# Channel attention with a squared-ReLU network behind it: a third buffer for rectified pairs and for split scores, nine for tokens, fewer for weights; all plain stores on SP's queue; a scheduler that assumes longer transfers

## The chip, the cores and the metric

One core of a Trainium2 chip runs the whole program. The metric is the device time of one execution in microseconds (us). PE is TensorE with its matmuls, PEld its weight loads, DVE is VectorE, ACT is ScalarE, POOL is GpSimd and SP is SyncE, which computes nothing here and issues transfers. All five work through their own instructions strictly in order, so an instruction that waits for a semaphore holds everything behind it on its engine.

## The reference

```
B, N, C = 4, 6080, 256
qn = q / (norm(q, axis=1) + 1e-06);  kn = k / (norm(k, axis=1) + 1e-06)
s = kn.transpose(0, 2, 1) @ qn / tau              # per batch 256 x 256
a = softmax(s, axis=-1)
x = (v @ a).reshape(24320, 256)
h = x @ w_in                                      # 256 -> 2048
g = maximum(h, 0) ** 2
out = g @ w_out                                   # 2048 -> 256
```

## The kernel before

**The work.** Attention is folded into the first weight: for each of the four batches `fold` multiplies the batch's 256 x 256 attention matrix by `w_in`, so the tokens `v` go straight into the network. Numbers are split into a high and a low part (`split`: a cast, then a subtraction on DVE), and each product is three matmuls, in the trace 128 x 128 weights by 512 or 480 columns. The tokens of a batch are cut into six chunks (five of 2 x 512 tokens, one of 2 x 480), 24 in all; the hidden layer is cut into eight blocks `j`. A chunk and a block make a "quad" (`quads`, 192 of them), and a quad's first layer is done with seven products instead of eight (`m1` to `m7`, weights `wt`, tokens `vt`).

**One quad.** The order of products on PE is m1, m7, some second-layer products, m6, m2, more of the second layer, m5, m4, more, m3 (`steps_of`). m1 goes into a PSUM bank of ring `h`, and ACT copies it to a bank `x` (`COPY x<-h`) before m6 may add to the first bank; m6's copy goes to `z`; m7 takes the second `h` bank and ACT copies it to SBUF (`m7`, shown as `m`). ACT rectifies m2 and m3 into a pair (ring `s`), DVE's line 704 adds `m7` to m4 and m5 and rectifies them (ring `s`, or `D` in the blocks that spare a product in the second layer too). A pair is squared on ACT, then split into high and low (ring `g2`), which the second layer reads one or two quads later with weights `wo`. The blocks in `GROUPS` also form sums of weights and of pairs (`load_later`, `split_later`, `run_later`: tiles `wo<-wod_M...`, `hl`, `kq`, results `uM...`), and the results leave through `outT<-uM` stores on SP's queue.

**Weights by way of DRAM.** A batch's folded weights are combined and split on ACT and DVE into a tile of ring `wt` (`combine`), stored to DRAM (`wsc`), and loaded again into the same ring of three buffers for each chunk (`load_wt`). Second-layer weights and the sums of them are prepared once (`wop`, `wos`, `wod`) and loaded for each quad into ring `wo`. While a batch's chunks run, the next batch's scores are computed: `kq` tiles are loaded, squared on ACT, added to `acc` by a DMA that accumulates (POOL's queue), split into ring `hl`, and multiplied.

**The order.** Nothing is ordered by hand. `Plan.order` simulates five engines (SP and POOL as "S" and "G", which only issue) and takes at each step the operation that is ready: for PE, SP and POOL the one with the smallest key, for ACT and DVE the one with the earliest due time. An operation starts only if its tiles' rings have a free buffer. Two estimates of a transfer go in: `delay` (from which due times are worked out backward) and, in the forward pass, `link` and `done`, the time at which readers may start. Operations that ACT or DVE can do (casts) go to whichever takes them first. So numbers in `RINGS` and in the estimates move instructions on all engines.

```
                    if e in "SG":
                        link = max(link, now + 0.8) + op.size / 330.0
                        done = link + 1.4
...
    RINGS = {"kq": 4, "g2": 3, "D": 3, "hl": 2, "t4": 1, "s": 2, "sq": 2, "wo": 6, "wt": 3, "vt": 8, "v": 1, "tt": 1,
```

Of the kernel before, what the change touches and what calls it, by code (L numbers as in the profile page):

```python
# [24 lines left out]
class Plan:  # L25
# [19 lines left out]
    def add(self, key, engines, fn, r=(), w=(), size=0):  # L45
        op = Op()
        op.engines, op.fn, op.key, op.size, op.n = engines, fn, key, size, len(self.ops)
        op.deps, op.users, op.tiles = set(), set(), set()
        for t in r:
            if t in self.writer:  # L50
                op.deps.add(self.writer[t])
            self.readers.setdefault(t, []).append(op)
        for t in w:
            op.deps.update(self.readers.pop(t, ()))
            if t in self.writer:
                op.deps.add(self.writer[t])
            self.writer[t] = op
        op.deps.discard(op)
        for t in (*r, *w):
            if t[0] in self.ring_of and t[0] not in op.tiles:  # L60
                op.tiles.add(t[0])
                self.users[t[0]].append(op)
        self.ops.append(op)
        return op
# [2 lines left out]
        return min(op.engines.values())  # L67

    def delay(self, op, e):
        return 2.2 + op.size / 330.0 if e in "SG" else self.LAT[e]  # L70

    def order(self):

# [21 lines left out]
        for op in reversed(ops):  # L95
            due = op.due if "P" in op.engines else end
            e = next(iter(op.engines))
# [22 lines left out]
        link = 0.0  # L120
        now = 0.0
        out = []
        seq = 0
        while events:
            now = heapq.heappop(events)
            while events and events[0] <= now + 1e-9:
                heapq.heappop(events)
            while ends and ends[0][0] <= now + 1e-9:
                op = heapq.heappop(ends)[2]
                for name in op.tiles:  # L130
                    open_[name] -= 1
                    if not open_[name] and name in live:
                        free[live.pop(name)] += 1
            progress = True
            while progress:
                progress = False
                for e in engines:
                    if at[e] > now + 1e-9:
                        continue
                    while head < len(pe) and pe[head] in begun:  # L140
                        head += 1
                    place = pe[head].key if head < len(pe) else 1e9
                    best = None
                    for op in waiting[e]:
                        if op.ready > now + 1e-9 or op.key > place + self.ahead[e]:
                            continue
                        rank = (op.key, op.n) if e in "PSG" else (
                            op.due + self.shy.get(e, 0.0) * (len(op.engines) > 1), op.n)
                        if best is not None and rank >= best[0]:
                            continue  # L150
                        need = {}
                        for name in op.tiles:
                            if name not in live:
                                need.setdefault(self.ring_of[name], []).append(turn[name])
                        if any(free[ring] < len(n) or ring not in self.loose and max(n) >= served[ring] + len(n)
                               for ring, n in need.items()):
                            continue
                        best = rank, op
                    if best is None:
                        continue  # L160
                    op = best[1]
                    for x in op.engines:
                        waiting[x].remove(op)
                    begun.add(op)
                    for name in op.tiles:
                        if name not in live:
                            live[name] = self.ring_of[name]
                            free[live[name]] -= 1
                            served[live[name]] += 1
                    op.begun = now  # L170
                    out.append((op, e))
                    at[e] = now + op.engines[e]
                    done = at[e] + self.LAT.get(e, 0.0)
                    if e in "SG":
                        link = max(link, now + 0.8) + op.size / 330.0
                        done = link + 1.4
                    seq += 1
                    heapq.heappush(events, at[e])
                    heapq.heappush(events, done)
                    heapq.heappush(ends, (done, seq, op))  # L180
                    for u in op.users:
                        u.left -= 1
                        u.ready = max(u.ready, done)
                        if not u.left:
                            for x in u.engines:
                                waiting[x].append(u)
                            heapq.heappush(events, u.ready)
                    progress = True
# [23 lines left out]
def tile_channel_attention_relu2_ffn(ctx, tc, kq, vT, tau, w_in, w_out, outT):  # L212
# [12 lines left out]
    G = 2  # L225
# [3 lines left out]
    GROUPS = ((0, 1, 2), (4, 5))  # L229
    SJ = sum(GROUPS, ())  # L230
    BIG = 3.4028234663852886e38
    RINGS = {"kq": 4, "g2": 3, "D": 3, "hl": 2, "t4": 1, "s": 2, "sq": 2, "wo": 6, "wt": 3, "vt": 8, "v": 1, "tt": 1,
             "m7": 2, "uM1": 1, "uM5": 1, "uM6": 1, "uM7": 1, "acc": 1, "s_acc": 1, "zq": 1, "e": 2, "den": 2,
             "aT": 1, "y": 3, "nm": 2,
             "h": 2, "x": 1, "z": 1, "o00": 1, "o01": 1, "o10": 1, "o11": 1}
    plan = Plan(RINGS, {"P": 0.7, "A": 1.2, "V": 1.2, "S": 2.0, "G": 2.0}, ("h",))
    add = plan.add
# [18 lines left out]
    def get(name, shape=None, dtype=F32):  # L256
        if name not in made:
# [5 lines left out]
            else:  # L263
                pool = small if ring in ("acc", "s_acc", "zq", "e", "den", "aT", "y", "nm") else work
                made[name] = pool.tile(shape, dtype, name=ring, tag=name[-1] if ring in ("aT", "y") else ring,
                                       bufs=1 if ring == "y" else RINGS[ring])
        return made[name]
# [29 lines left out]
    def load(key, out, in_, r, w, size):  # L297
        add(key, {"S": 0.45}, lambda e: nc.sync.dma_start(out=out(), in_=in_()), r, w, size)

    def store(key, out, in_, r, w, size, e="G"):  # L300
        add(key, {e: 0.45 if e == "S" else 1.0},
            lambda e: (nc.sync if e == "S" else nc.gpsimd).dma_start(out=out(), in_=in_()), r, w, size)

# [55 lines left out]
    def decode_w_in(key, g, lead=0.9):  # L359
        Wn = decode(key, "in", g, "sq" if g else "t4", lead)  # L360
        win[0, g] = Wn
        store(key, lambda: dtile(("wins", g), [P, 4, GW]), lambda: made[Wn], [(Wn, 0)], [(("wins", g), 0)], 512)
# [723 lines left out]
```

## Time and profile before

| | |
|---|---|
| time, median of 3 runs | 2133.39 us (2130.94 to 2135.16) |
| the profiled execution's own time | 2129.49 us |
| its span on the core | 2127.6 us |
| PE busy | 2097.1 us, 99% of the span |
| DVE, ACT, POOL busy | 1950.4, 1557.0, 93.8 us |
| DMA traffic | 495.84 MB, 233 GB/s on average |

The profiled execution lies 3.9 us under the median. Matmuls overlap one another in the records, so a busy PE need not be a PE at full pace. POOL computes nothing after the start: its queue issues stores and accumulating transfers.

### The profile page before, as it was taken

What the parts mean: (1) busy time and instruction counts of PE and PEld (TensorE: products, weight loads), DVE (VectorE), ACT (ScalarE), POOL (GpSimd) and SP (SyncE); (2) the same over time, 40 slices, a digit from 0 to 9 for tenths busy, and PEclk for the clock granted to TensorE, in tenths of its full rate; (3) what the DMA queues carried; (4) which work ended last, traced back from release to release, by engine and by line L of the source; (5) the groups of instructions that cost most, each with busy time, mean ns of one, the idle gap of its engine ahead of it and who ended that gap; (6) DMA issues with size and microseconds to landing.
All of it is one profiled execution on the core that took longest, in us unless ns stands there. A gap on an engine that the chain in (4) does not pass through costs nothing. (4 is left out here: it accounts for less than half of the span.)

```text
span 2127.6 us, 27875 instructions
## 1 busy us (share of the span) xinstructions
PE 2097.1 (99%) x9566; PEld 1736.8 (82%) x9566; DVE 1950.4 (92%) x3074; ACT 1557.0 (73%) x2402; POOL 93.8 (4%) x127
## 2 busy tenths in 40 slices
PE   8999999999999999999999999999999999999999
PEld 7778888787888888888887888888878788888887
DVE  7898799999999999999998999998999999899897
ACT  6677777876787777777777777777777676676765
POOL 0113000000000000000000000000000000000000
PEclk9999999999999999999999999999999999999999
DMA  9769656466788887846668889785666665565553
GB/s 366 294 229 336 243 205 223 146 222 219 273 301 260 249 280 235 251 172 224 216 241 291 268 246 283 227 241 191 222 223 212 240 223 176 200 219 177 197 201 100
DMA packets 150796, 495.84 MB, mean 233 GB/s; under 512 B 15264, under 2 KB 47520, under 8 KB 150656
## 3 DMA queue, kind: packets, MB, share of 16 engines
q1 hardware_dynamic: 136096, 429.71, 58.2%
q0 software_dynamic: 14560, 64.36, 10.6%
q8 instruction: 76, 1.25, 0.2%
q14 instruction: 64, 0.52, 0.1%
HBM read 404.75 MB, written 65.14 MB: 221 GB/s over the span
## 5 line engine op out<-in xcount | busy, mean ns | idle before, releaser
L811 PE MATMUL o<-g,wo 128*128 128x512 f32 (+1 forms) x2628 | 688.1, 388 | 0.5 <-DVE g L295 0.5
L666 PE MATMUL h<-vt,wt 128*128 128x512 f32 (+1 forms) x2304 | 627.8, 391 | 14.4 <-DMA wt<-wsc 4.9
L811 PEld LDWEIGHTS o<-g,wo 128*128 128x128 f32 x2628 | 490.1, 188 | 97.7 <-DVE g L295 1.1
L666 PEld LDWEIGHTS h<-vt,wt 128*128 128x128 f32 x2304 | 426.2, 188 | 116.6 <-ACT x L270 12.8
L274 ACT ACTIVATE s<-s 128x1024 f32<-128x1024 f32 (+1 forms) x274 | 288.4, 1053 | 113.7 <-DVE s L704 112.9
L295 DVE TENSOR_TENSOR g<-s,g 128x1024 fp32r<-128x1024 f32 (+1 forms) x274 | 331.1, 1208 | 15.4 <-ACT g L270 14.3
L666 PE MATMUL z<-vt,wt 128*128 128x512 f32 (+1 forms) x1152 | 325.0, 390 | 4.4 <-DVE s L704 3.4
L811 PE MATMUL h<-hl,wo 128*128 128x512 f32 (+1 forms) x1056 | 295.6, 389 | 0.0
L666 PEld LDWEIGHTS z<-vt,wt 128*128 128x128 f32 x1152 | 211.9, 188 | 50.9 <-DVE s L704 7.6
L295 DVE TENSOR_TENSOR hl<-D,hl 128x512 fp32r<-128x512 f32 (+1 forms) x352 | 232.8, 680 | 1.1 <-ACT hl L270 0.7
L811 PEld LDWEIGHTS h<-hl,wo 128*128 128x128 f32 x1056 | 197.9, 188 | 41.4 <-DVE s_acc L432 0.7
L270 ACT CAST hl<-D 128x512 fp32r<-128x512 f32 (+1 forms) x259 | 152.5, 616 | 65.4 <-PE h L811 38.8
L274 ACT ACTIVATE D<-D 128x1024 f32<-128x1024 f32 (+1 forms) x110 | 115.4, 1049 | 107.3 <-DVE D L704 107.2
L666 PE MATMUL x<-vt,wt 128*128 128x512 f32 (+1 forms) x576 | 161.4, 388 | 0.0
L280 ACT ACTIVATE s<-z 128x512 f32<-128x512 f32 (+1 forms) x192 | 112.4, 585 | 55.4 <-PE z L666 54.9
L270 DVE CAST g<-s 128x1024 fp32r<-128x1024 f32 (+1 forms) x160 | 109.7, 686 | 29.1 <-ACT s L274 28.5
L666 PEld LDWEIGHTS x<-vt,wt 128*128 128x128 f32 x576 | 108.4, 188 | 22.1
L270 ACT COPY z<-h 128x512 f32<-128x512 f32 (+1 forms) x192 | 111.1, 578 | 17.8 <-PE h L666 17.0
L270 ACT COPY x<-h 128x512 f32<-128x512 f32 (+1 forms) x192 | 111.0, 578 | 12.0 <-PE h L666 8.8
L280 ACT ACTIVATE s<-x 128x512 f32<-128x512 f32 (+1 forms) x192 | 113.9, 593 | 7.5 <-PE x L666 1.8
L270 ACT CAST g<-s 128x1024 fp32r<-128x1024 f32 (+1 forms) x114 | 118.7, 1041 | 0.7
L270 ACT COPY m<-h 128x512 f32<-128x512 f32 (+1 forms) x192 | 110.7, 577 | 6.1 <-PE h L666 3.6
(145 smaller groups left out, 2757.2 us busy)
## 6 DMA issues: line engine op xcount, KB each, us to landing
wt<-wsc SPq DMA_DIRECT2D x184, 896.0 KB, 5.4
kq<-kq SPq DMA_DIRECT2D x87, 512.0 KB, 6.4
wo<-wos SPq DMA_DIRECT2D x110, 384.0 KB, 4.6
wo<-wop SPq DMA_DIRECT2D x74, 512.0 KB, 4.1
wo<-wod_M SPq DMA_DIRECT2D x88, 384.0 KB, 5.4
wsc<-wt POOLq DMA_DIRECT2D x32, 896.0 KB, 5.6
acc<-sq POOLq DMA_DIRECT2D x46, 512.0 KB, 7.7
wo<-wod_M SPq DMA_DIRECT2D x88, 256.0 KB, 2.7
```

Source lines behind the costliest of these rows:

```text
L270: (nc.scalar.copy if e == "A" else nc.vector.tensor_copy)(out=out, in_=in_)
L274: nc.scalar.activation(out=out, in_=in_, func=AF.Square)
L280: nc.scalar.activation(out=out, in_=in_, func=AF.Relu)
L295: add(key, {"V": vec(n)}, lambda e: nc.vector.tensor_sub(out=l(), in0=x(), in1=h()), (*r, *wh), wl)
L666: nc.tensor.matmul(out=out[:, :T], lhsT=made[w][:, l, i], rhs=made[v][:, r, :T], start=start and n == 0, stop=n == 2, skip_group_check=True)
L811: nc.tensor.matmul(out=o[:, :T], lhsT=l, rhs=x[:, :T], start=start and k == 0, stop=stop and k == 2)
```

## The change

The scheduler's two estimates of a transfer grow: a transfer on SP's queue by 1.0 us, one on POOL's by 4.0 us, each time beside its size over 330. The rings `hl`, `s` and `vt` get one buffer more, `g2` and `m7` one less, `wo` two less. Stores that took POOL's queue by default now take SP's; the accumulating transfers stay on POOL's.

```
     def delay(self, op, e):
-        return 2.2 + op.size / 330.0 if e in "SG" else self.LAT[e]
+        return (3.2 if e == "S" else 6.2) + op.size / 330.0 if e in "SG" else self.LAT[e]
...
                         link = max(link, now + 0.8) + op.size / 330.0
-                        done = link + 1.4
+                        done = link + (2.4 if e == "S" else 5.4)
...
-    RINGS = {"kq": 4, "g2": 3, "D": 3, "hl": 2, "t4": 1, "s": 2, "sq": 2, "wo": 6, "wt": 3, "vt": 8, "v": 1, "tt": 1,
-             "m7": 2, "uM1": 1, "uM5": 1, "uM6": 1, "uM7": 1, "acc": 1, "s_acc": 1, "zq": 1, "e": 2, "den": 2,
+    RINGS = {"kq": 4, "g2": 2, "D": 3, "hl": 3, "t4": 1, "s": 3, "sq": 2, "wo": 4, "wt": 3, "vt": 9, "v": 1, "tt": 1,
+             "m7": 1, "uM1": 1, "uM5": 1, "uM6": 1, "uM7": 1, "acc": 1, "s_acc": 1, "zq": 1, "e": 2, "den": 2,
...
-    def store(key, out, in_, r, w, size, e="G"):
+    def store(key, out, in_, r, w, size, e="S"):
```

The change moves instructions on every engine. Three places are shown; numbers behind names tell tiles apart and differ between the two programs.

First, the last two stores of folded weights for the third batch (`wsc6`, `wsc7`), with what stands around them. Before, on SP's queue:

```order
L298 DMA v_10438<-vT 128x1024 x2
L298 DMA wo_10448<-wod_M5_1417 128x768
L298 DMA wt_10482<-wsc2_9627 128x1792
L298 DMA kq_10495<-kq 128x1024
L302 DMA outT<-uM6_10032 128x480
L302 DMA outT<-uM1_9886 128x480
L298 DMA wo_10540<-wop_3_775 128x1024
L298 DMA wt_10553<-wsc3_9756 128x1792
L302 DMA outT<-uM7_10093 128x480
L298 DMA wo_10601<-wod_M6_1426 128x768
L298 DMA wt_10641<-wsc4_9994 128x1792
```

and on POOL's, with the accumulating transfers of the next batch's norms among the stores:

```order
L302 DMA wsc5_10074<-wt_10046 128x1792
L302 DMA wsc6_10430<-wt_10330 128x1792
L398 DMA acc_10366<-sq_10466 128x1024
L398 DMA acc_10366<-sq_10546 128x1024
L302 DMA wsc7_10584<-wt_10480 128x1792
```

Now both stores stand on SP's queue:

```order
L302 DMA wsc6_10397<-wt_10272 128x1792
L298 DMA v_10416<-vT 128x1024 x2
L298 DMA wo_10437<-wod_M1_1332 128x768
L298 DMA kq_10467<-kq 128x1024
L298 DMA wt_10475<-wsc2_9610 128x1792
L302 DMA wsc7_10496<-wt_10464 128x1792
L302 DMA outT<-uM6_10035 128x480
L298 DMA wo_10530<-wos_2_1532 128x2x384
L302 DMA outT<-uM1_9912 128x480
L298 DMA wt_10559<-wsc3_9688 128x1792
L302 DMA outT<-uM7_10094 128x480
L298 DMA wt_10582<-wsc4_9991 128x1792
```

Before, `wt_10482` waits for the landing of store `wsc6` and `wt_10641` for that of `wsc7`, because they take the stored tiles' buffers; `wsc7` itself stands behind two accumulating transfers. Now of the loads shown only `wt_10582` takes the buffer of a stored tile (`wsc7`'s), and no accumulating transfer is ahead of either.

Second, PE in the third batch's weight stage, from the first product of a quad (`h_9280` before, `h_9266` now) to the product that must wait for ACT's copy of that bank (the second row of the same bank). Before:

```order
L666 MATMUL h_9280<-vt_8330,wt_9164 128x512 x3
L811 MATMUL h_9258<-kq_9206,wo_9088 128x512 x3
L811 MATMUL o01_9212<-g2_9208,wo_8959 128x512 x3
L666 MATMUL h_9280<-vt_8711,wt_9164 128x512 x3
L666 MATMUL h_9306<-vt_8705,wt_9164 128x512 x3
```

Now:

```order
L666 MATMUL h_9266<-vt_8324,wt_9145 128x512 x3
L811 MATMUL h_9258<-hl_9183,wo_9167 128x512 x3
L811 MATMUL o00_8950<-g2_9204,wo_9095 128x512 x3
L811 MATMUL h_9258<-kq_9212,wo_9167 128x512 x3
L811 MATMUL o01_9215<-g2_9204,wo_9095 128x512 x3
L666 MATMUL h_9266<-vt_8699,wt_9145 128x512 x3
L666 MATMUL h_9303<-vt_8458,wt_9145 128x512 x3
```

Two products stood between the first use of the bank and the second; now there are four.

Third, SP's queue in a chunk of the last batch, where no stores of weights are left: the loads of second-layer weights (`wo`) among those of first-layer weights (`wt`). Before:

```order
L298 DMA wo_17133<-wos_5_1744 128x2x384
L298 DMA wo_17201<-wod_M5_1417 128x512
L298 DMA wt_17219<-wsc7_15477 128x1792
L298 DMA wo_17251<-wod_M6_1426 128x512
L298 DMA wo_17294<-wop_6_1227 128x1024
L298 DMA wt_17306<-wsc0_14200 128x1792
L298 DMA wo_17348<-wod_M7_1435 128x512
```

Now:

```order
L298 DMA wt_17218<-wsc7_15469 128x1792
L298 DMA wo_17250<-wos_5_1784 128x2x384
L298 DMA wo_17296<-wod_M5_1416 128x512
L298 DMA wt_17306<-wsc0_14188 128x1792
L298 DMA wo_17350<-wod_M6_1421 128x512
L298 DMA wo_17358<-wop_6_1273 128x1024
L298 DMA wo_17387<-wod_M7_1424 128x512
```

The loads of `wos_5` and `wod_M5` have moved behind that of `wsc7`, those of `wod_M6` and `wop_6` behind that of `wsc0`: with four buffers a `wo` tile comes free later.

## Rows read from the trace of the kernel before

**Rows 1.** The page's head and busy times.

```profile
span 2127.6 us, 27875 instructions
PE 2097.1 (99%) x9566; PEld 1736.8 (82%) x9566; DVE 1950.4 (92%) x3074; ACT 1557.0 (73%) x2402; POOL 93.8 (4%) x127
```

**Rows 2.** PE's waits: engine, line, releaser: us in total, times, longest.

```profile
PE h L666 <- DMA wt<-wsc: 4.9, 3, 3.3
PE h L666 <- ACT x L270: 4.5, 6, 1.1
...
PE z L666 <- DVE s L704: 3.4, 5, 1.7
PE h L666 <- DVE uM L854: 2.3, 5, 0.6
```

**Rows 3.** The same of the weight loads.

```profile
PEld h L666 <- ACT x L270: 12.8, 19, 1.6
PEld z L666 <- DVE s L704: 7.6, 12, 2.2
PEld h L666 <- DVE uM L854: 6.7, 11, 1.0
PEld h L666 <- ACT uM L270: 6.1, 13, 0.5
```

**Rows 4.** Windows: length, busy time (instructions) by engine, clock, DMA share, GB/s.

```profile
1124.00:1128.00 4.00, 4.00 (x20) 3.36 (x19) 4.00 (x7) 3.58 (x7) 0.87 (x1) 1.00 0.96 341
1132.00:1152.00 20.00, 15.42 (x65) 12.07 (x65) 15.11 (x26) 13.50 (x19) 2.27 (x3) 0.91 1.02 337
1148.00:1152.00 4.00, 4.00 (x12) 2.96 (x11) 1.14 (x2) 3.78 (x6) 0.00 (x0) 0.58 1.03 310
```

**Rows 5.** Timelines of POOL's and SP's issues there: start, duration, issue.

```profile
1121.54 0.54 POOL L302 DMA_DIRECT2D wsc<-wt  x1 [36.89 <-PE h L666]
...
1135.19 0.56 POOL L302 DMA_DIRECT2D wsc<-wt  x1
...
1121.67 0.38 SPq L298 DMA_DIRECT2D wo<-wod_M  x1
1130.32 0.33 SPq L298 DMA_DIRECT2D wt<-wsc  x1
...
1137.98 0.32 SPq L298 DMA_DIRECT2D wo<-wod_M  x1
1147.41 0.32 SPq L298 DMA_DIRECT2D wt<-wsc  x1
```

**Rows 6.** Who waited for stores of folded weights, whole span.

```profile
SPq L298 <- DMA wsc<-wt: 75.5, 17, 9.4
...
ACT wt L270 <- DMA wsc<-wt: 11.1, 9, 2.3
```

**Rows 7.** ACT's and PE's timelines in the same batch's weight stage.

```profile
1044.22 0.41 ACT L270 CAST wt<-kq 128x256 fp32r<-128x256 f32 x1 [1.80 <-DMA wsc<-wt]
1044.53 0.55 ACT L270 COPY x<-h 128x480 f32<-128x480 f32 x1
...
1045.14 0.92 PE L666 MATMUL h<-vt,wt 128*128 128x480 f32 x3 [0.63 <-ACT x L270]
```

**Rows 8.** DMA issues: queue, count, size, median us from issue to landing.

```profile
wt<-wsc SPq DMA_DIRECT2D x184, 896.0 KB, 5.4
...
wo<-wos SPq DMA_DIRECT2D x110, 384.0 KB, 4.6
...
wsc<-wt POOLq DMA_DIRECT2D x32, 896.0 KB, 5.6
...
wo<-wod_M SPq DMA_DIRECT2D x88, 256.0 KB, 2.7
```

**Rows 9.** The view of tile `wo`: all its transfers, issue to landing.

```profile
DMA to landing us min/median/max: 2.2/4.4/13.1
```

**Rows 10.** The chain that ended last, in a chunk of the last batch: start, us, what.

```profile
1796.44 1.36 PE o L811 x6
```

## The prediction

> **What bounds the kernel.** I read the page first: PE is busy for 2097.1 of 2127.6 us [rows 1], so only 30.5 us are plainly idle. Nothing in this change takes a matmul away (the order has as many now as before), so all that can be won are pauses, and the question is which of them the new order closes and which it opens. DVE is at 92% and ACT at 73%: neither bounds the whole, but both are in order, and when one stands, PE follows within a product or two.
>
> The second view is who waits for whom. PE's list [rows 2] names few causes: loads of folded weights (4.9 us), ACT's copy of the first product (4.5), DVE's additions (3.4 and 2.3). The weight loads' list [rows 3] has the same causes with larger sums, because a load waits while earlier matmuls still run. The time really lost lies between the two rows of a cause: for ACT's copy between 4.5 and 12.8 us.
>
> The third view is the one place where PE is plainly starved. Windows there [rows 4] show 20 matmuls in the 4 us from 1124 and 65 in the 20 us from 1132, where five times 20 would be 100. 35 are missing, at 0.2 us each 7.0 us. In the last 4 us of them, after PE had stood still, the granted clock was 0.58, so most of that stretch ran at the lower of the two levels (1.2 GHz instead of 2.4) and held 12 matmuls; that loss is inside the 7.0 us.
>
> Why PE starves there is in the timelines [rows 5]. SP issued at 1121.67 and then nothing until 1130.32: the next load takes the buffer of a stored weight tile, and that store, issued by POOL at 1121.54, had to land. What had piled up behind it then went out in a bunch, and after 1137.98 SP stood again until 1147.41, for the store that POOL could issue only at 1135.19, behind accumulating transfers. The DMA engines were full meanwhile (share 1.02 [rows 4]), so the bunched loads came late. Over the span SP stood for such stores 75.5 us in 17 waits, ACT 11.1 us in 9 [rows 6]. One of the latter is shown [rows 7]: ACT stood 1.80 us before a cast into a `wt` buffer, the copy `x` behind it came late, and PE waited 0.63 us.
>
> **The change part by part.** The sum is made against the profiled execution's 2129.5 us; the median of the runs shown is 3.9 us above it, and I add that at the end. A measurement of this kernel can tell about 0.2% (4.3 us) from no change.
>
> *Stores on SP's queue, longer transfers assumed (weights by way of DRAM).* 74 stores leave POOL. Their issue costs SP about 0.55 us each by POOL's own rows [rows 5], or 41 us of a queue that stood still for 8 and 9 us at a time; SP does nothing else, so this costs nothing unless a load is just behind. What matters is how far a load stands from the store that it must wait for. Counted in the order, in matmuls on PE at 0.227 us each (six in 1.36 us [rows 10]), between what the store waits for and what the load would wait for otherwise, the two stores at the place in rows 5 had 4.6 and 4.8 us before and have 12.0 and 8.0 us now. The store takes 5.6 us to land in the median [rows 8], and 8.8 and 12.2 us at this place (1121.54 to about 1130.3, 1135.19 to about 1147.4, when the waiting load goes out [rows 5]). So SP's two stops of 8.7 and 9.4 us should shrink to at most a few us, and with them the bunching. From below nothing is won (if the DMA engines are full anyway), from above the 7.0 us. I take 5, nearer to the upper end since the stops cause the bunch, and nothing for the same places in the other two batches: **-5 us**.
>
> On this point the Trainium skill speaks against the change: "DMA: Bandwidth & Descriptors", section "Issuing engines are not separate DMA queues", says that transfers issued from different engines share the same 16 engines, and that another issuer saves only issue time. The row on landings bears that out: 896 KB take 5.6 us from POOL and 5.4 from SP [rows 8]. By that rule alone a store at this place would land as late as before (12.2 us against a distance of 8.0), SP would still stand some 4 us, and I would write -2 instead of -5. I keep -5 because the gain comes from the order, which POOL's accumulating transfers no longer delay.
>
> *Copies and sums that PE waits for.* The order gives PE more room. Counted over all 192 quads, the number in which at most two products (1.36 us) stand between m1 and m6 falls from 110 to 59; three or more rise from 82 to 133. That is the room for ACT's copy, which takes 0.55 us and waits behind whatever ACT is doing. So waits for this copy should fall by about 46%: of the 8.7 us in the middle of the two rows [rows 2, 3] 4.0 us. The bounds are 2.1 (46% of 4.5) and 5.9 (of 12.8). The other causes of this kind (DVE's rectified sums, `uM` by DVE and ACT: 3.4, 2.3 and nothing on PE, 7.6, 6.7 and 6.1 on its loads) are not tied to a count that I can make. A third `s` and `hl` buffer lets a square or a split wait for its reader without holding the next one. I take -2 of some 13 (the middle of the sums 5.7 and 20.4), with bounds of +3 and -8. Together **-6 us**.
>
> *Four `wo` buffers instead of six.* The distance between the last matmul on the old tile and the first on the new one, counted in the same way, was at least 13.0 us in all 358 such loads; now it is under 11 us in 139 of 360, under 9 in 31, and 7.5 at the least. Landing takes 4.4 us in the median and 13.1 at the most over all loads of `wo` [rows 9], so most are still in time, but waiting stores ahead of them (`outT` behind DVE's sums) eat some of it. Below: nothing. Above: all 139 late by 0.2 us, 28. I take one in five of the 31 tight ones late by 0.5 us: **+3 us**.
>
> *Stores and splits again.* The longer estimate is 5.9 us for a folded-weight store where the old one was 4.9, and the planner now places the next tile's first cast 5.4 to 6.8 us behind the store's inputs at four places of each batch; before, three or four places stood at 5.9 to 11.6. The median landing is 5.6 us, so some waits as in rows 7 stay and a few may come anew: ±2, taken as nothing.
>
> *The rest at nothing.* A second `m7` buffer is not needed: the m7 product takes the second `h` bank, which is free only when DVE has read the previous quad's other bank together with `m7`; without that cover it would be one addition of DVE per quad. The third `g2` buffer held splits that the second layer reads a quad later; now the squared pair waits in the third `s`. The ninth `vt` lets one more token split run ahead at a chunk's start. Casts move between ACT and DVE in both directions (18 wide ones leave DVE, of the narrow ones 54 come and 34 leave), so DVE's load stays about as it is.
>
> Sum: -5 - 6 + 3 = -8, so 2121.5 by the profile and **2125 us** as a median (2133.4 - 8).
>
> **The rivals.**
>
> *The gain is larger (chance 0.17).* If the two stops of SP end wholly (-7), the pauses for copies and sums are halved throughout (half of 21.7, the middle of 10.2 on PE and 33.2 on its loads: -11) and no `wo` load is late, it is -18: 2115. For it: the counted room. Against it: the m6 waits that cost most came after ACT had stood for a store [rows 7], not from little room.
>
> *No change (0.20).* The stops move. A store on SP's queue waits for ACT's and DVE's last split, and the loads behind it wait too; before, that wait was POOL's alone. Where the split is 2 us late, some `wt` or `wo` load is 2 us late, and if every tenth load behind the 32 stores is as late, that gives back 6 to 10 us: 2131 to 2135, say 2133. Against it: the loads behind a store have 8 us and more.
>
> *Slower (0.16).* The four `wo` buffers decide. SP cannot issue a `wo` load before the old tile's last matmul, the DMA engines can be full for 20 us on end [rows 4], and the slowest such load took 13.1 us [rows 9]. If 60 of the 139 loads with under 11 us come 0.4 us late, that is +24 against the -11 of the other terms: +13, 2146. It decides from about 40 loads on that are late by 0.4 us (16 us: the -11 and another 4.3). For it: the least room falls from 13.0 to 7.5 us at one stroke. Against it: most of these loads are of 256 and 384 KB, with medians of 2.7 and 4.6 us [rows 8].
>
> **How the numbers follow.** My forecast, -4.3 to -13 (2120 to 2129), has 0.47, the larger gain (under 2120) 0.17, no change 0.20, slower 0.16. Faster by over 0.2% is 0.47 + 0.17 = 0.64. The range from 2112 to 2139 takes in most of the larger gain, all of no change, and the near part of slower; what lies outside is the far end of the `wo` case and of the gain.
>
> **What would show it.** Right: SP's waits for `wsc<-wt` fall well under 75.5 us, windows around 1130 to 1150 us hold some 20 matmuls in 4 us at full clock, the PE rows for ACT's `x` halve, and PE's busy total does not grow. Wrong: a row of PE or its loads that waits for `DMA wo<-wod` or `wo<-wos` with more than a few us (there is none now among PE's), or ACT and DVE rows for `wsc<-wt` above 11.1 us. If the time falls but SP still stands for stores as long, the copies carried it; if the copies' rows stay and it falls, the stores did.

## The result and the profile after

The changed kernel takes 2099.85 us (median of four runs, 2097.51 to 2102.27) against 2132.16 us for the kernel before (2130.57 to 2135.16). The ratio is 0.9847, with a 95% interval from 0.9827 to 0.9866: 32 us faster where 8 were forecast, and below the range of 2112 to 2139. The profiled execution took 2097.62 us.

The head and busy times of the page after:

```profile
span 2095.9 us, 27701 instructions
PE 2081.4 (99%) x9566; PEld 1741.4 (83%) x9566; DVE 1941.9 (93%) x3076; ACT 1574.3 (75%) x2400; POOL 41.6 (2%) x53
```

The same 9566 matmuls fit into 31.7 us less. Only half of that was visible as idle time before: PE's idle time falls from 30.5 to 14.5 us, but its busy time falls too, from 2097.1 [rows 1] to 2081.4. Matmul records overlap: in the quiet stretch below, a record lasts 390 ns in the mean and the next one starts 227 ns behind it (the median), so a matmul that starts 100 ns late leaves no idle time. So "busy" contained 15.7 us of lost pace, a small part of it at the lower clock (0.91 in the starved 20 us [rows 4]).

What is left on PE's own list of waits (engine, line, releaser: us in total, times, longest):

```profile
PE x L423 <- DMA kq<-kq: 3.6, 1, 3.6
PE h L488 <- DVE zq L480: 2.6, 1, 2.6
PE h L557 <- DVE s L704: 1.1, 2, 1.0
PE h L666 <- ACT x L270: 0.9, 1, 0.9
PE z L666 <- ACT z L270: 0.8, 2, 0.4
PE h L666 <- DVE uM L854: 0.7, 2, 0.4
PE z L557 <- DVE aT L295: 0.2, 1, 0.2
```

The loads of folded weights (4.9 us [rows 2]) are gone from it, ACT's copy `x` went from 4.5 to 0.9, DVE's line 704 in front of `z` from 3.4 to nothing. The weight loads' list says the same of the copy:

```profile
PEld h L666 <- DVE uM L854: 3.1, 9, 0.8
...
PEld h L666 <- ACT x L270: 3.0, 5, 1.3
```

3.0 stands for 12.8, and 3.1 for 6.7 [rows 3]. The other two rows shown there are gone: DVE's line 704 in front of `z` (7.6) and ACT's copy `uM` in front of `h` (6.1).

Windows show where the pace came back (length, busy time and instructions by engine, granted clock, DMA share, GB/s): an early stretch, the starved stretch of the prediction, and a quiet one in the last batch, with neither stores of weights nor scores. Before:

```profile
70.00:200.00 130.00, 126.19 (x550) 102.25 (x549) 113.30 (x178) 98.35 (x151) 25.64 (x39) 1.00 0.76 284
...
1729.00:1995.00 266.00, 265.07 (x1163) 217.51 (x1163) 240.07 (x376) 185.12 (x291) 0.00 (x0) 1.00 0.60 203
```

After:

```profile
70.00:200.00 130.00, 128.06 (x562) 104.79 (x561) 110.40 (x171) 102.82 (x157) 0.00 (x0) 1.00 0.79 283
1132.00:1152.00 20.00, 20.00 (x100) 16.83 (x99) 20.00 (x31) 15.66 (x24) 1.73 (x2) 1.00 0.84 269
1729.00:1995.00 266.00, 266.00 (x1174) 219.78 (x1173) 240.86 (x377) 193.14 (x298) 0.00 (x0) 1.00 0.59 196
```

The starved 20 us now hold 100 matmuls, not 65, at full clock [rows 4]: 35 times 0.2 us, the 7.0 us of the prediction. The surprise is the quiet stretch. PE was idle there for 0.93 of 266 us, and yet 11 matmuls more now fit in, which at 266/1174 = 0.227 us each are 2.5 us, or 0.95%. The starts of the matmuls show where: before, 12 of them come 0.34 to 0.78 us behind the one ahead, together 2.6 us over the usual 0.227; after, three come 0.3 us behind. PE's own list hardly names this loss. The list of the weight loads does; its rows between 1700 and 2000 us, before:

```profile
PEld h L666 <- ACT x L270: 2.4, 4, 0.8
PEld h L666 <- ACT uM L270: 2.1, 4, 0.5
```

After, this is all that is left there:

```profile
PEld h L666 <- DVE uM L854: 0.9, 4, 0.2
```

4.5 us of waiting for ACT's copies became 0.9 for DVE's sums. The number of matmuls in a fixed window, a reading that the prediction lacked, tells what such rows are worth.

A pace 0.95% better over the whole span would be 20 us, but the span is not like this throughout. Both kernels start the same 9566 matmuls, so the start of the n-th in one trace can be set beside that of the n-th in the other. The kernel before ends 32.1 us behind. It loses 20.4 us of this in the three stages in which folded weights are made and stored (430 to 650, 945 to 1160 and 1460 to 1670 us of the changed kernel), 2.2 in the first 150 us, and 9.5 in the other 1296 us, where the quiet stretch lies.

SP's queue around the same place (start, duration, issue):

```profile
1102.29 0.32 SPq L302 DMA_DIRECT2D wsc<-wt  x1
...
1113.28 0.33 SPq L302 DMA_DIRECT2D wsc<-wt  x1
...
1119.05 0.33 SPq L298 DMA_DIRECT2D wt<-wsc  x1
...
1121.59 1.25 SPq L298 DMA_DIRECT2D wt<-wsc  x1
```

The last two stores of the batch leave at 1102.29 and 1113.28, where POOL issued them at 1121.54 and 1135.19 [rows 5], and the loads behind no longer stand for 8.7 and 9.4 us. Most of the difference between these times is not the stores' own: the changed kernel is already 14 us ahead there (its 5001st matmul starts at 1092.2 us, the old kernel's at 1106.0). The waits for such stores over the span:

```profile
SPq L298 <- DMA wsc<-wt: 20.0, 9, 3.7
...
ACT wt L270 <- DMA wsc<-wt: 2.0, 4, 0.7
```

75.5 and 11.1 us were there before [rows 6].

### The profile page after: what moved, and what is told of

The parts are those of the page before. It is cut to its first block, busy times and chain, and to the rows that moved or that the text cites. A ratio compares the mean times of both kernels' runs of the same rounds, so it can differ in the third digit from the quotient of the medians.

```text
span 2095.9 us, 27701 instructions
## 1 busy us (share of the span) xinstructions
PE 2081.4 (99%) x9566; PEld 1741.4 (83%) x9566; DVE 1941.9 (93%) x3076; ACT 1574.3 (75%) x2400; POOL 41.6 (2%) x53
## 4 chain that ended last, share of the span: by engine, by line
PE 92%; DVE 4%; ACT 2%; DMA 1%; issue 1%; SPq 0%; ACTq 0%; DVEq 0%
PE o L811 30%; PE h L666 24%; PE h L811 14%; PE z L666 12%; PE x L666 6%; PE h L423 4%; PE h L557 2%; PE x L423 1%; DMA wsc<-wt 0%; DVE s L704 0%; DVE hl L295 0%; DMA vt<-w_in 0%; DMA wt<-wsc 0%; DVE wt L295 0%; ACT s L274 0%
## 5 line engine op out<-in xcount | busy, mean ns | idle before, releaser
L666 PE MATMUL h<-vt,wt 128*128 128x512 f32 (+1 forms) x2304 | 620.2, 389 | 1.7 <-ACT x L270 0.9
L270 ACT CAST hl<-D 128x512 fp32r<-128x512 f32 (+1 forms) x226 | 134.6, 615 | 36.8 <-PE h L423 23.5
L270 ACT CAST g<-s 128x1024 fp32r<-128x1024 f32 (+1 forms) x129 | 134.1, 1040 | 14.7 <-PE o L811 13.5
L270 DVE CAST g<-s 128x1024 fp32r<-128x1024 f32 (+1 forms) x145 | 99.0, 683 | 17.2 <-ACT s L274 13.4
```

The source lines that it names most:

```text
L270: (nc.scalar.copy if e == "A" else nc.vector.tensor_copy)(out=out, in_=in_)
L666: nc.tensor.matmul(out=out[:, :T], lhsT=made[w][:, l, i], rhs=made[v][:, r, :T], start=start and n == 0, stop=n == 2, skip_group_check=True)
```

## The experiments

The theory after the result: most of the gain is pace over the whole span and comes from the third buffer of ring `s` (pairs of `m2` and `m3`, and of the blocks outside `GROUPS`), while the stores and the estimates end only the waits for stores. The table at the end of this section shows how far that holds. The first rival: stores and estimates carry it, and the rings add little. The second: the gain comes with the third `hl` buffer, which the pairs do not use. Each ratio below is to the kernel before on the same chip, with its 95% interval; a hundredth is 21 us.

**The three parts alone.** The estimates alone:

```
-        return 2.2 + op.size / 330.0 if e in "SG" else self.LAT[e]
+        return (3.2 if e == "S" else 6.2) + op.size / 330.0 if e in "SG" else self.LAT[e]
...
-                        done = link + 1.4
+                        done = link + (2.4 if e == "S" else 5.4)
```

> The kernel before with the longer transfer estimates alone (rings and queues as before). Theory 'estimates' (the new order places casts and loads so late that nobody stands for a transfer, and this carries most of the 32 us): ratio 0.988 to 0.993. Theory 'buffers' (the third s and hl and the ninth vt let ACT and DVE run ahead, and this carries it): 0.998 to 1.003. Theory 'queue' (stores must leave POOL's accumulating transfers): 0.998 to 1.003 too.

2122.72 us, 0.9945 (0.9930 to 0.9959).

SP's queue for stores alone:

```
-    def store(key, out, in_, r, w, size, e="G"):
+    def store(key, out, in_, r, w, size, e="S"):
```

> The kernel before with its stores on SP's queue alone. Theory 'queue': ratio 0.988 to 0.995, and SP's waits for the stores of folded weights fall well under 75 us. 'Estimates' and 'buffers': 0.997 to 1.003, those waits stay.

2120.27 us, 0.9934 (0.9919 to 0.9949).

All six rings alone:

```
-    RINGS = {"kq": 4, "g2": 3, "D": 3, "hl": 2, "t4": 1, "s": 2, "sq": 2, "wo": 6, "wt": 3, "vt": 8, "v": 1, "tt": 1,
-             "m7": 2, "uM1": 1, "uM5": 1, "uM6": 1, "uM7": 1, "acc": 1, "s_acc": 1, "zq": 1, "e": 2, "den": 2,
+    RINGS = {"kq": 4, "g2": 2, "D": 3, "hl": 3, "t4": 1, "s": 3, "sq": 2, "wo": 4, "wt": 3, "vt": 9, "v": 1, "tt": 1,
+             "m7": 1, "uM1": 1, "uM5": 1, "uM6": 1, "uM7": 1, "acc": 1, "s_acc": 1, "zq": 1, "e": 2, "den": 2,
```

> The kernel before with the new ring sizes alone. Theory 'buffers': ratio 0.986 to 0.992, PE's waits for copies and sums (about 26 us between the two lists) fall by more than half. 'Estimates' and 'queue': 0.996 to 1.005, with four wo buffers perhaps a loss.

2111.62 us, 0.9891 (0.9874 to 0.9907). The rings are the largest part, 23 us. Each of the other two is worth 12 to 14 us alone, more than the 5 that the prediction gave both. The starved stretch shows that all three close the same hole, each in its own way. The estimates, then SP's queue, then the rings, in the same 20 us:

```profile
1132.00:1152.00 20.00, 18.41 (x84) 14.35 (x83) 19.25 (x32) 15.77 (x25) 3.14 (x4) 1.00 1.01 311
```

```profile
1132.00:1152.00 20.00, 19.96 (x99) 16.64 (x98) 19.75 (x33) 16.21 (x25) 1.72 (x2) 1.00 1.04 357
```

```profile
1132.00:1152.00 20.00, 20.00 (x97) 16.73 (x97) 19.95 (x33) 16.38 (x26) 1.71 (x2) 1.00 1.01 335
...
1729.00:1995.00 266.00, 266.00 (x1174) 219.76 (x1173) 242.31 (x380) 196.07 (x304) 0.00 (x0) 1.00 0.60 201
```

84, 99 and 97 matmuls where there were 65. How long SP stands for stores over the span does not tell the gain: 16.7 us with the estimates alone, 42.2 with SP's queue alone and 42.4 with both. Only the rings raise the quiet stretch to 1174; estimates and SP's queue leave it at 1163 each, as before.

**Two of three.** The first without the rings, the second without SP's queue, the third without the estimates, each as a difference from the changed kernel:

```
-    RINGS = {"kq": 4, "g2": 2, "D": 3, "hl": 3, "t4": 1, "s": 3, "sq": 2, "wo": 4, "wt": 3, "vt": 9, "v": 1, "tt": 1,
-             "m7": 1, "uM1": 1, "uM5": 1, "uM6": 1, "uM7": 1, "acc": 1, "s_acc": 1, "zq": 1, "e": 2, "den": 2,
+    RINGS = {"kq": 4, "g2": 3, "D": 3, "hl": 2, "t4": 1, "s": 2, "sq": 2, "wo": 6, "wt": 3, "vt": 8, "v": 1, "tt": 1,
+             "m7": 2, "uM1": 1, "uM5": 1, "uM6": 1, "uM7": 1, "acc": 1, "s_acc": 1, "zq": 1, "e": 2, "den": 2,
```

> The changed kernel with the old ring sizes (so estimates and queue alone). Theory 'buffers': ratio to the kernel before 0.996 to 1.002, the copies' and sums' waits come back. 'Estimates' or 'queue' or the two together: 0.985 to 0.990.

2120.37 us, 0.9934 (0.9919 to 0.9949).

```
-    def store(key, out, in_, r, w, size, e="S"):
+    def store(key, out, in_, r, w, size, e="G"):
```

> The changed kernel with its stores left on POOL's queue (new rings and estimates). If rings and one remedy for the store waits are enough (theory 'two kinds of pauses': rings close those for copies and sums, either estimates or queue those for stores): ratio to the kernel before 0.983 to 0.988. Theory 'each adds its own': 1 - 0.0109 - 0.0055, so 0.9836, and the changed kernel would be 0.6% faster than this one, which it is not if the first theory holds.

2105.80 us, 0.9878 (0.9863 to 0.9892).

```
-        return (3.2 if e == "S" else 6.2) + op.size / 330.0 if e in "SG" else self.LAT[e]
+        return 2.2 + op.size / 330.0 if e in "SG" else self.LAT[e]
...
-                        done = link + (2.4 if e == "S" else 5.4)
+                        done = link + 1.4
```

> The changed kernel with the old estimates (new rings, stores on SP). Theory 'two kinds of pauses': 0.983 to 0.988, like e5_nosp. Theory 'each adds its own': 1 - 0.0109 - 0.0066, so 0.9825. If estimates are needed to order for the new queue: 0.990 or above, with waits for stores on SP, ACT or DVE.

2103.37 us, 0.9868 (0.9852 to 0.9883). Estimates and SP's queue together (0.9934) give no more than SP's queue alone (0.9934): they are two remedies for the same waits. On top of the rings, either adds 0.13 to 0.23 points, with intervals that overlap, and both 0.44 (0.9891 to 0.9847). The first rival falls: without the rings 18 of 32 us are missing.

**Which ring.** First the changed kernel with one buffer less, of `s` and of `hl`:

```
-    RINGS = {"kq": 4, "g2": 2, "D": 3, "hl": 3, "t4": 1, "s": 3, "sq": 2, "wo": 4, "wt": 3, "vt": 9, "v": 1, "tt": 1,
+    RINGS = {"kq": 4, "g2": 2, "D": 3, "hl": 3, "t4": 1, "s": 2, "sq": 2, "wo": 4, "wt": 3, "vt": 9, "v": 1, "tt": 1,
```

> The changed kernel with two s buffers. If the third buffer for rectified pairs is what closes the pauses for copies and sums: ratio to the kernel before 0.991 to 0.996, near the changed kernel with all old rings (0.9934), and weight loads' waits for ACT's x and DVE's sums come back. If hl or vt carries it: 0.984 to 0.988.

2120.65 us, 0.9949 (0.9933 to 0.9966).

```
-    RINGS = {"kq": 4, "g2": 2, "D": 3, "hl": 3, "t4": 1, "s": 3, "sq": 2, "wo": 4, "wt": 3, "vt": 9, "v": 1, "tt": 1,
+    RINGS = {"kq": 4, "g2": 2, "D": 3, "hl": 2, "t4": 1, "s": 3, "sq": 2, "wo": 4, "wt": 3, "vt": 9, "v": 1, "tt": 1,
```

> The changed kernel with two hl buffers. If the third hl buffer carries the ring gain: ratio to the kernel before 0.991 to 0.996. If the third s buffer does: 0.984 to 0.988.

2116.98 us, 0.9926 (0.9910 to 0.9942). Both cost much, 1.0 and 0.8 points, but in different places. Two `s` buffers, early and quiet stretch, and the weight loads' waits between 1700 and 2000 us:

```profile
70.00:200.00 130.00, 126.17 (x551) 102.44 (x549) 111.47 (x176) 95.95 (x148) 0.00 (x0) 1.00 0.77 271
...
1729.00:1995.00 266.00, 263.74 (x1160) 216.91 (x1159) 241.38 (x379) 191.26 (x297) 0.00 (x0) 1.00 0.58 199
...
PEld h L666 <- ACT x L270: 4.7, 4, 1.2
PEld h L811 <- ACT uM L270: 0.7, 4, 0.2
```

Two `hl` buffers:

```profile
70.00:200.00 130.00, 124.37 (x533) 101.72 (x532) 108.55 (x174) 97.69 (x151) 0.00 (x0) 0.97 0.72 260
...
1729.00:1995.00 266.00, 266.00 (x1174) 219.79 (x1173) 245.08 (x381) 191.94 (x303) 0.00 (x0) 1.00 0.60 204
```

Without the third `s` the quiet stretch falls back to 1160, the early one to 551, and the weight loads wait for ACT's `x` again. This goes for all runs: the seven kernels with two `s` have such a row for `x` between 1700 and 2000 us (1.6 to 4.7 us) and 1160 to 1171 matmuls in the quiet stretch, and of the eleven with three `s` none has it, and they have 1173 or 1174. Without the third `hl` it stays at 1174, and the early stretch loses 29 of 562 matmuls, 6.6 us at 0.227 each. There the first batch's attention matrix is folded into `w_in` (line 557), whose split parts stand in ring `hl`, while the network's weights are decoded through two tiles of the same ring (`decode`). PE's list of that kernel names the place, and a `wo` load besides:

```profile
PE h L557 <- ACT m L270: 4.6, 2, 2.8
...
PE o L811 <- DMA wo<-wop: 3.4, 1, 3.4
```

Then each alone on the kernel before, a `wo` buffer or two given up for the room:

```
-    RINGS = {"kq": 4, "g2": 3, "D": 3, "hl": 2, "t4": 1, "s": 2, "sq": 2, "wo": 6, "wt": 3, "vt": 8, "v": 1, "tt": 1,
+    RINGS = {"kq": 4, "g2": 3, "D": 3, "hl": 2, "t4": 1, "s": 3, "sq": 2, "wo": 5, "wt": 3, "vt": 8, "v": 1, "tt": 1,
```

> The kernel before with a third s buffer alone (one wo buffer less makes room). Theory 'two buffers, two stages': the third s closes the copies' pauses of the plain chunks, so the 266 us from 1729 hold 1174 matmuls instead of 1163 (some 2.3 us in each 266, 15 to 18 us over the span), while the stages that store weights keep their stops: ratio 0.992 to 0.996. Theory 's and hl only work together': 0.997 to 1.003, and 1163 matmuls.

2115.25 us, 0.9914 (0.9897 to 0.9931).

```
-    RINGS = {"kq": 4, "g2": 3, "D": 3, "hl": 2, "t4": 1, "s": 2, "sq": 2, "wo": 6, "wt": 3, "vt": 8, "v": 1, "tt": 1,
+    RINGS = {"kq": 4, "g2": 3, "D": 3, "hl": 3, "t4": 1, "s": 2, "sq": 2, "wo": 4, "wt": 3, "vt": 8, "v": 1, "tt": 1,
```

> The kernel before with a third hl buffer alone (two wo buffers less make room). Theory 'two buffers, two stages': splits and so stores of folded weights come earlier, PE is no longer starved near 1140 us (-5 to -7 us), the plain chunks stay at about 1160 matmuls: ratio 0.995 to 0.999. Theory 's and hl only work together': 0.998 to 1.003.

2136.81 us, 1.0021 (1.0010 to 1.0031). One buffer of `s`, with nothing else but a `wo` buffer less, gives 18 us, over half of the whole gain. Its quiet stretch, and over the whole span what the weight loads and PE still wait for, of the four causes that the prediction summed as copies and sums:

```profile
1729.00:1995.00 266.00, 266.00 (x1174) 219.71 (x1173) 245.83 (x383) 189.94 (x300) 0.00 (x0) 1.00 0.59 199
...
PEld h L666 <- DVE uM L854: 4.9, 8, 1.3
...
PEld h L666 <- ACT x L270: 3.1, 7, 0.9
...
PE h L666 <- DVE uM L854: 2.5, 3, 0.9
...
PE h L666 <- ACT x L270: 0.5, 1, 0.5
```

Line 704 in front of `z` and ACT's `uM` in front of `h` (7.6 and 6.1 us on the weight loads before) have no row here either. With that the second rival falls as the main cause: 18 us come without a third `hl`, which also rules out that the two only work together, although the ratio with `hl` alone is the one which that theory asked for. What `hl` is worth by itself the second kernel cannot tell, since it also gives up two `wo` and ends a little slower. Its early stretch holds 563 matmuls, as in the changed kernel, so the buffer does its work there. Its quiet stretch is the best of those with two `s`, and it loses in the starved one:

```profile
1132.00:1152.00 20.00, 15.88 (x66) 13.02 (x65) 13.69 (x21) 13.00 (x21) 2.28 (x3) 0.83 0.95 309
1729.00:1995.00 266.00, 266.00 (x1171) 218.97 (x1171) 247.53 (x388) 177.96 (x281) 0.00 (x0) 1.00 0.58 202
```

ACT and DVE stand longer for stores there; their rows for stores over the whole span:

```profile
ACT wt L270 <- DMA wsc<-wt: 23.3, 9, 5.0
...
DVE wt L270 <- DMA wsc<-wt: 12.1, 5, 3.7
```

**The price of fewer buffers.** The changed kernel with eight `vt`; the same with five `wo`; and the changed kernel with two `hl` and six `wo`:

```
-    RINGS = {"kq": 4, "g2": 2, "D": 3, "hl": 3, "t4": 1, "s": 3, "sq": 2, "wo": 4, "wt": 3, "vt": 9, "v": 1, "tt": 1,
+    RINGS = {"kq": 4, "g2": 2, "D": 3, "hl": 3, "t4": 1, "s": 3, "sq": 2, "wo": 4, "wt": 3, "vt": 8, "v": 1, "tt": 1,
```

> The changed kernel with eight token buffers. If the ninth does nothing: ratio to the kernel before 0.982 to 0.987, as the changed kernel. If it lets the token splits of the next chunk run ahead in a way that PE needs: 0.988 or more.

2107.63 us, 0.9876 (0.9854 to 0.9898).

```
-    RINGS = {"kq": 4, "g2": 2, "D": 3, "hl": 3, "t4": 1, "s": 3, "sq": 2, "wo": 4, "wt": 3, "vt": 9, "v": 1, "tt": 1,
+    RINGS = {"kq": 4, "g2": 2, "D": 3, "hl": 3, "t4": 1, "s": 3, "sq": 2, "wo": 5, "wt": 3, "vt": 8, "v": 1, "tt": 1,
```

> The changed kernel with eight token buffers and five wo buffers in their place. If four wo buffers cost what the prediction charged for them (+3 us), this is 1 to 3 us faster than e11_vt8; if they cost nothing, the two are equal within 2 us.

2100.74 us, 0.9846 (0.9829 to 0.9863).

```
-    RINGS = {"kq": 4, "g2": 2, "D": 3, "hl": 3, "t4": 1, "s": 3, "sq": 2, "wo": 4, "wt": 3, "vt": 9, "v": 1, "tt": 1,
+    RINGS = {"kq": 4, "g2": 2, "D": 3, "hl": 2, "t4": 1, "s": 3, "sq": 2, "wo": 6, "wt": 3, "vt": 9, "v": 1, "tt": 1,
```

> The changed kernel with two hl and six wo buffers. If e8_hl2 (0.9926) lost by its four wo buffers when the DMA engines were full: ratio to the kernel before 0.984 to 0.988, and no pauses near 613 and 1158. If the third hl buffer itself is needed: 0.990 to 0.994.

2107.59 us, 0.9885 (0.9868 to 0.9901). Here the `wo` loads do bite. With eight `vt` and four `wo`, the first row of PE's list is of the kind that the prediction named as a sign (it named loads from `wod` and `wos`; this one is from `wop`):

```profile
PE o L811 <- DMA wo<-wop: 5.0, 2, 2.6
```

The fifth `wo` buffer takes that row away and wins 7 us; the fifth and sixth together, with two `hl`, win 9 (2116.98 to 2107.59). In the changed kernel itself no wait of PE names `wo`, and the landings are not slower than before; the view of tile `wo` says

```profile
DMA to landing us min/median/max: 2.5/3.9/11.4
```

against 2.2, 4.4 and 13.1 [rows 9]. So the ninth `vt`, worth 6 us by the ratios (0.9876 to 0.9847, intervals overlapping), seems to have its worth through the order of the loads: with it four `wo` buffers are enough, and without it five give the changed kernel's ratio. No kernel beat that.

The reductions alone, on the kernel before:

```
-    RINGS = {"kq": 4, "g2": 3, "D": 3, "hl": 2, "t4": 1, "s": 2, "sq": 2, "wo": 6, "wt": 3, "vt": 8, "v": 1, "tt": 1,
-             "m7": 2, "uM1": 1, "uM5": 1, "uM6": 1, "uM7": 1, "acc": 1, "s_acc": 1, "zq": 1, "e": 2, "den": 2,
+    RINGS = {"kq": 4, "g2": 2, "D": 3, "hl": 2, "t4": 1, "s": 2, "sq": 2, "wo": 4, "wt": 3, "vt": 8, "v": 1, "tt": 1,
+             "m7": 1, "uM1": 1, "uM5": 1, "uM6": 1, "uM7": 1, "acc": 1, "s_acc": 1, "zq": 1, "e": 2, "den": 2,
```

> The kernel before with the smaller rings alone (two g2, four wo, one m7). If wo's four buffers cost as charged: ratio 1.001 to 1.003 with a row of PE waits for DMA of wo. If the smaller rings cost nothing: 0.999 to 1.001.

2140.91 us, 1.0041 (1.0025 to 1.0057), 9 us slower. PE's first row there is not `wo` but the folded weights, with nearly twice the 4.9 us of before:

```profile
PE h L666 <- DMA wt<-wsc: 8.3, 4, 2.8
```

**Adding up from the third pair buffer.** The kernel with `s` 3 and `wo` 5, now with SP's queue for stores, and then with the estimates too:

```
-    def store(key, out, in_, r, w, size, e="G"):
+    def store(key, out, in_, r, w, size, e="S"):
```

> The kernel before with a third s buffer (five wo) and stores on SP's queue, nothing else. Theory 'two separate gains': 1 - 0.0086 - 0.0066, so 0.983 to 0.987, as the changed kernel. If hl is needed besides: 0.989 to 0.993.

2107.76 us, 0.9886 (0.9871 to 0.9900).

```
-        return 2.2 + op.size / 330.0 if e in "SG" else self.LAT[e]
+        return (3.2 if e == "S" else 6.2) + op.size / 330.0 if e in "SG" else self.LAT[e]
...
-                        done = link + 1.4
+                        done = link + (2.4 if e == "S" else 5.4)
```

> The same with the longer estimates. If the estimates are a second remedy for the same waits: within 0.2% of e14_s3sp. If they add their own: 0.3 to 0.5% faster.

2105.99 us, 0.9877 (0.9862 to 0.9892). In ratios times 2132 us the steps from before to after are -18 (third `s`), -6 (SP's queue), -2 (estimates) and -6 (the other rings together), in sum -32. The intervals of single steps reach 3 to 4 us either way, so the -2 is not told from nothing.

**Where each part gains.** How far each kernel falls behind the changed one, by the start of the n-th matmul as above, in us. Each row is one profiled execution, and executions of one kernel differ by up to 8 us, so single figures are rough; the third `s` alone is 12.3 better than the kernel before here and 18 by the medians.

| kernel | first 150 us | three weight stages, 645 us | the rest, 1296 us | all |
|---|---|---|---|---|
| before | 2.2 | 20.4 | 9.5 | 32.1 |
| estimates alone | 6.8 | 9.6 | 10.6 | 27.0 |
| SP's queue alone | 4.3 | 7.1 | 11.3 | 22.7 |
| both, old rings | 4.3 | 7.5 | 10.6 | 22.4 |
| third `s` alone | 4.8 | 12.9 | 2.1 | 19.8 |
| all rings alone | 2.9 | 12.1 | -0.2 | 14.8 |
| changed, two `s` | 2.7 | 4.9 | 14.6 | 22.3 |
| changed, two `hl` | 9.9 | 11.4 | 1.9 | 23.2 |

The last column but one goes by `s`: 9.5 us or more with two, 2.1 or less with three. So the theory holds for where the third `s` works and not for how much that is: the pace outside the weight stages is a third of the whole gain. The weight stages hold the larger part, and there the third `s` and the two remedies for the stores each take 7 to 13 of the same 20 us.

## Why the prediction was wrong

The direction was right; the size was not. Step by step:

**"What can be won are pauses", 30.5 us.** The idle time is half of what was lost: it fell by 16.0 us, the busy time by 15.7. The other half was in the second view of the prediction, in the longer list of the weight loads; its remark that the time really lost lies between the two lists came true. So this step did not make the forecast small: -8 lies far under 30.5.

**Copies and sums, -6.** This is the step that failed most, by its size and not by its mechanism. The third `s` alone measured -18 and its removal from the changed kernel cost 21 us (2120.65 to 2099.85), where the whole term was -6 and its bound on that side -14 (-5.9 and -8). The prediction's own two lists held the larger figure. Its four causes (ACT's `x`, line 704 in front of `z`, `uM` by DVE and by ACT) stood at 10.2 us on PE and 33.2 on its loads; they stand at 1.6 and 6.1 in the changed kernel, so the middle fell by 17.9 us. With the third `s` alone they stand at 3.0 and 8.0, a fall of 16.2. (The remedies for the stores help `x` too: its row on the loads falls from 12.8 to 5.4 us with the estimates alone and to 5.9 with SP's queue alone.) Of `x` the prediction asked for 4.0 of 8.7 us, and 6.7 went (8.7 to 2.0). Of the other three it asked for "-2 of some 13", with no count behind it, and 11 went: this is the part that was mis-sized.

The counted room does follow the third buffer, if not neatly: of the 192 quads, those with at most two products between m1 and m6 number 110 before and 59 after; of the kernels counted, those with a third `s` have 58 to 71 and 1173 or 1174 matmuls in the quiet stretch, and those with two have 95 to 111 and 1160 to 1171. That the room is what makes the pace is argued from this count and not shown by itself; the kernel with 99 such quads has 1160, the one with 111 has 1165, so the count does not order them. How long ACT stands for its squares does not order them either. Its rows in the last batch (1700 to 2000 us), first of the changed kernel with two `s` and then of the one with three `s` and the rest as before:

```profile
ACT s L274 <- DVE s L704: 17.6, 12, 2.5
```

```profile
ACT s L274 <- DVE s L704: 15.5, 8, 2.8
```

nearly the same wait, with 1160 and 1174 matmuls beside it. (The third `s` takes some 16 us off this wait each time: 31.5 in the kernel before against these 15.5, and these 17.6 against 2.0 in the changed kernel.) What does order them is the weight loads' wait for ACT's `x`. What is shown is that the third buffer of `s` ends this wait, by adding and by taking it away; which of ACT's operations it moves out of the copy's way stays open.

**Stores on SP's queue and the estimates, -5.** The mechanism was right in the main: SP's waits for stores went from 75.5 to 20.0 us, the starved stretch got its 7.0 us back and the granted clock stayed at 1.00. The size was short: -12 and -14 for either alone, -14 together; on top of the third `s` about -8, since the rings close part of the same stretch. The prediction priced one place and gave nothing, without a reason, for the same places in the other two batches. SP's queue alone takes 7.6 us from the priced weight stage (10.3 to 2.7 us behind the changed kernel), close to the 7.0 of its bound, and 5.8 from the other two (4.4 to 1.7 and 5.8 to 2.7). The Trainium skill's rule that another issuer saves only issue time ("DMA: Bandwidth & Descriptors", section "Issuing engines are not separate DMA queues") holds for the transfer itself only in part. The loads and stores of the changed kernel, and then the stores of the kernel with SP's queue alone:

```profile
wt<-wsc SPq DMA_DIRECT2D x184, 896.0 KB, 5.7
...
wsc<-wt SPq DMA_DIRECT2D x32, 896.0 KB, 6.2
```

```profile
wsc<-wt SPq DMA_DIRECT2D x32, 896.0 KB, 5.1
```

The prediction set a store from POOL beside a load from SP, which are not the same transfer. As stores, 6.2 us is a little above POOL's 5.6 [rows 8], but there rings and estimates differ too. Where the queue alone differs, the median store lands sooner from SP's queue in four pairs of kernels of five: 5.1 us for 5.6 (the kernel before), 5.4 for 6.6 (with the estimates), 4.9 for 5.7 (with the rings), 4.2 for 5.4 (with the third `s`), 6.2 for 6.1 (with rings and estimates). Some 0.2 us of it is the issue (0.54 us on POOL's queue, 0.32 on SP's); the cause of the rest is not shown. The -2 that the prediction worked out by that rule is still far from the -14 of SP's queue alone. That the gain lies in the store's place is argued from the orders: it no longer stands in POOL's queue behind accumulating transfers, and the planner puts more between it and the load that needs its buffer. That the distance counts and POOL's queue is no bar is shown by the estimates alone, which leave every store on POOL's queue and give 12 us.

**Four `wo` buffers, +3.** Nothing of it shows in the changed kernel; the rival that made it decide the time did not come. But the mechanism is real in its neighbours, at 7 to 9 us, where the order lets a `wop` load fall into a stretch with busy DMA engines (share 0.96 between 1130 and 1155 us with eight `vt`). Of the nine kernels with four `wo`, two have a row for it over 3 us, so its absence is the luck of an order and not a property of four buffers.

**"The rest at nothing".** Wrong by about 6 us in the chain of steps above. Taken from the changed kernel, the third `hl` is worth 17 us (0.9926 to 0.9847), of which 9 come back with six `wo` (0.9885), and the ninth `vt` 6 us. The single buffers of `m7` and the two of `g2` were not run apart, so what they cost alone stays open; with four `wo` and no new buffer they are part of +9 us.

**Stores and splits, nothing.** The rows of ACT for stores fell from 11.1 to 2.0 us, so this term should have been a small gain.

**The rivals.** "The gain is larger" was the case that came, with a chance of 0.17 and 2115 us; its two parts (the stops end, the pauses are halved) both happened, and it still was 15 us too high: the pauses for copies and sums fell by four fifths and not by half, and the stores gained in all three weight stages. The measured time lies below this case too, so its chance says little.

## What to carry to other kernels

Where PE is 99% busy with overlapping matmuls, count the matmuls per window in a quiet stretch and in the best one, and read the waits of the weight loads before those of the matmuls: the idle time saw half of the loss here, and the loads' list named the cause of the rest. Set the starts of the n-th matmuls of two kernels side by side before a gain in one window is carried over to the span: 0.95% in the quiet stretch would have been 20 us, and 9.5 lay there. A ring that an engine beside the bounding one fills and empties in order (here the rectified pairs) can set the pace through that engine's other work (here the copy `x`), so look at its depth early, and pay for it from a ring whose loads have time to spare. Two remedies for one wait do not add up; price the second on top of the first.

## What the runs showed of the hardware

Full DMA engines need not starve PE. With SP's queue alone the DMA share between 1132 and 1152 us is 1.04 (1.02 before [rows 4]) and 99 matmuls run where 65 did, with the rings alone 1.01 and 97; what hurt was the order in which the loads waited, and not the traffic.

A store of 896 KB took 5.6 us in the median in the kernel before, from POOL's queue, 5.1 with SP's queue alone, and 6.2 from SP's queue in the changed kernel; loads of the same size took 5.4, 5.5 and 5.7, and the span's mean traffic was 233, 234 and 237 GB/s.
